# Attention and max-of-two network on one core: loading batch 0's q and k in two parts by tokens

## The chip, the cores and the metric

The kernel runs on one core of a Trainium2 chip. The metric is device time in microseconds (us), from the first to the last instruction. Most runs of a kernel agree within 0.3%. The kernel before gives 282.1 to 283.4 us in nearly all of its runs (two took 284.1); one run of 705.16 us stands alone and is not used.

Names: TensorE (PE) multiplies matrices and transposes, ScalarE (ACT) does the exponentials, VectorE (DVE) and GpSimd (POOL) copy, cast and mask, SyncE (SP) issues loads. POOL also issues loads, in the same line of instructions as its casts and masks.

## The reference, cut to what matters

```python
# q, k, v: (8 batches, 8 heads, 576 tokens, 64), each randn * 0.1
scores = (1 / sqrt(64)) * q @ k.T
mask = (row // 64) >= (col // 64)          # causal by blocks of 64
attn = softmax(where(mask, scores, -1e9)) @ v
x = attn as (4608 tokens, 512)
out = maximum(x @ w1, x @ w2) @ w_out      # w1, w2: 512 x 1024, w_out: 1024 x 512
```

With q and k scaled by 0.1, a score has a spread of about 0.1 x 0.1 x sqrt(64) / 8 = 0.01, so the softmax is nearly flat, and which token a score belongs to hardly shows in the output. "Correct" is therefore a weak statement here about the order of tokens in q and k.

## The kernel before

Heads go in pairs, pairs in groups of two; batch 0 is groups 0 and 1. One load brings q (or k) of a group, 64 x 2 partitions of 9 tokens each. It is cast to bf16, transposed on TensorE, and copied from PSUM.

```python
NP = 64; RPP = S // NP        # 9 tokens per partition
QCUT = 256                    # early queries: below token 256

def load_qk(g, queues, gated=False):
    ...
    raws[nm, g] = t = raw.tile([P, 2, RPP * D], FP32, name=f"{nm}raw")
    if gated:
        nc.gpsimd.memset(t[:, 0, :1], 0.0)      # holds the load back until POOL gets here
    queue.dma_start(out=t[:], in_=src[b, 4 * u:4 * u + 4].rearrange(
        "(s h) (p t) d -> (h p) s (t d)", h=2, t=RPP))

def load_v(b, c):   nc.gpsimd.dma_start(...)    # 128 tokens of all heads
def load_w(...):    nc.gpsimd.dma_start(...)    # columns of w1 and w2
def mask(p, a0, eng=None):
    (eng or nc.gpsimd).memset(aT_r[p % NA][BLK:, :, a0:a0 + BLK], 0.0)
def fill(n):        # n units of the first projection, as far as its tokens are done
def warm_up(n):     # n matmuls of 512 columns on zeros: nothing useful
```

The schedule of batch 0 is written out by hand. `burst_p` is the scores and exponential of a pair's early queries, `burst_q1` to `q3` of its late ones, `av` the product of attention and v (tiles 0, 1 early, 2 to 4 late), `x_out` the transposes of its result. Group 2 already belongs to batch 1.

```python
warm_up(16)
cq = transposes("q", 0, (dve, act)); ck = transposes("k", 0, (act, dve))
...
burst_p(0); masks_p(0); burst_p(1); warm_up(2); masks_p(1)
for c in range(2, NCH): load_v(0, c)            # POOL
load_w(256, 256)                                # POOL
...
cast("q", 2, ((pool, 0, RPP),)); masks_q(0); cast("k", 2, ((pool, 0, RPP),))
...
```

The softmax here doesn't subtract the row's maximum and nothing guards it: scores larger than these inputs give would overflow.

## Time and profile before

| | before |
|---|---|
| time, median | 283.12 us |
| TensorE busy | 96% of the span |
| first scores of batch 0 | 8.44 us |
| early k of group 1 cast on POOL | 9.17 us |
| attention times v, tiles 2 to 4, of pair 0 and pair 2 | 20.31 and 24.86 us |
| first scores of batch 1 | 27.06 us |

The prediction below shows the chain of waits, the stretches and the timelines. Columns: busy us and (count) of PE, weight loads, DVE, ACT and POOL, the granted clock, DMA share, GB/s.

```profile
0.00:8.30 8.30, 6.04 (x52) 2.50 (x52) 5.07 (x20) 2.76 (x5) 3.21 (x10) 1.00 0.78 281
8.30:16.00 7.70, 6.01 (x98) 3.17 (x101) 6.51 (x16) 6.06 (x10) 7.26 (x14) 1.00 1.52 258
```

Read the last column with the length of the stretch: 8.3 us at 281 GB/s are 2.33 MB, and 7.7 us at 258 are 1.99 MB, so 4.32 MB had come by 16 us.

The marks on TensorE's timeline are these (start us, busy us, then in brackets any idle time before and what ended it):

```profile
8.44 0.34 PE L321 MATMUL ps_s<-qT,kT 64*128 64x256 bf16 x4 [0.73 <-ACT kT L310]
...
20.31 0.90 PE L429 MATMUL ps_o<-vv,aT 128*128 128x65 bf16 x24
...
24.86 0.88 PE L429 MATMUL ps_o<-vv,aT 128*128 128x65 bf16 x24
...
27.06 0.61 PE L321 MATMUL ps_s<-qT,kT 64*128 64x512 bf16 x6
```

### The profile page before, as it was taken

The numbers are of one execution on the slowest core, as the hardware profiler recorded it, in microseconds if no ns is written. First come the engines' busy times: TensorE is split into PE (matmuls) and PEld (weight loads), VectorE is DVE, ScalarE is ACT, GpSimd is POOL, SyncE is SP. The second block draws the span as 40 slices with busy tenths as digits, with TensorE's granted clock in tenths as the row PEclk, the third lists the DMA queues.
The fourth block names the chain that finished last, engine by engine and source line by source line (L and its number), as shares of the span: only waits on it lengthen the run. The fifth ranks groups of instructions, "written<-read, shape, count | busy, mean of one in ns | idle before, by whom it ended". The sixth has DMA issues, their size and how long they took to land.

```text
span 280.4 us, 7767 instructions
## 1 busy us (share of the span) xinstructions
PE 269.3 (96%) x3208; PEld 151.5 (54%) x3253; DVE 185.7 (66%) x386; ACT 139.6 (50%) x194; POOL 107.7 (38%) x271
## 2 busy tenths in 40 slices
PE   7699999999999999999999999999999999999995
PEld 2356766655556455555555554646455644444543
DVE  5967879668887676767667576757655766365430
ACT  3786577667664664655647374664653000100112
POOL 2996446764654625164344625371120000000000
PEclk9999999999999999999999999999999999999999
DMA  7999999979934994479266866175301111111114
GB/s 261 263 219 220 187 244 273 250 148 189 210 42 153 154 156 78 178 82 239 49 208 77 219 75 196 52 81 50 67 5 49 49 54 40 39 75 40 73 41 150
DMA packets 55940, 36.68 MB, mean 131 GB/s; under 512 B 38752, under 2 KB 43232, under 8 KB 55904
## 3 DMA queue, kind: packets, MB, share of 16 engines
q0 software_dynamic: 41728, 7.87, 35.0%
q1 hardware_dynamic: 13760, 27.66, 28.8%
q10 hardware_dynamic: 416, 0.66, 0.7%
q8 instruction: 25, 0.41, 0.6%
q14 instruction: 11, 0.09, 0.1%
HBM read 34.60 MB, written 9.44 MB: 157 GB/s over the span
## 4 chain that ended last, share of the span: by engine, by line
PE 91%; DMA 4%; issue 2%; ACT 1%; DVE 1%; POOL 0%; ACTq 0%
PE ps_h L197 43%; PE ps_y L215 22%; PE ps_o L429 11%; PE ps_s L321 8%; DMA vv<-in_v_dram 2%; PE ps_xe L451 2%; PE ps_qT L303 2%; DMA qraw<-in_q_dram 2%; PE ps_kT L303 2%; ACT aT L345 1%; PE ps_s L339 1%; PE ps_y L231 1%; PE ps_w L292 1%; DVE g L206 0%; POOL vv L133 0%
## 5 line engine op out<-in xcount | busy, mean ns | idle before, releaser
L197 PE MATMUL ps_h<-xT,w_sb 128*128 128x512 bf16 (+3 forms) x605 | 136.2, 357 | 1.7 <-issue 0.3
L345 ACT ACTIVATE aT<-ps_s 128x1024 bf16<-128x1024 f32 (+2 forms) x100 | 96.2, 996 | 17.2 <-PE ps_s L321 16.2
L197 PEld LDWEIGHTS <-w_sb 128*128 128x128 bf16 x640 | 57.8, 98 | 57.4 <-issue 8.1
L204 DVE CAST h<-ps_h 128x512 bf16<-128x512 f32 (+3 forms) x80 | 50.9, 637 | 28.9 <-PE ps_h L197 26.7
L215 PE MATMUL ps_y<-wo_sb,g 128*128 128x512 bf16 x273 | 65.5, 379 | 2.1 <-PE ps_s L321 1.3
L206 DVE TENSOR_TENSOR g<-h,ps_h 128x512 bf16<-128x512 bf16 (+3 forms) x80 | 50.6, 632 | 12.0 <-PE ps_h L197 10.5
L350 POOL MEMSET aT<- 64x128 bf16 x124 | 22.3, 199 | 92.7 <-ACT aT L345 91.3
L221 ACT COPY y<-ps_y 128x512 f32<-128x512 f32 x31 | 18.1, 584 | 70.3 <-PE ps_y L215 56.5
L429 PEld LDWEIGHTS <-aT 128*128 128x128 bf16 x960 | 37.3, 98 | 14.1 <-issue 1.3
L215 PEld LDWEIGHTS <-g 128*128 128x128 bf16 x280 | 26.8, 98 | 30.4 <-issue 1.1
L429 PE MATMUL ps_o<-vv,aT 128*128 128x65 bf16 x960 | 39.9, 194 | 0.3 <-DMA vv<-in_v_dram 0.3
L133 POOL DMA_DIRECT2D vv<-in_v_dram x40 | 33.7, 847 | 0.5
L436 DVE TENSOR_TENSOR xp<-ps_o,rec 128x256 bf16<-128x256 f32 (+1 forms) x64 | 31.4, 491 | 2.2
L321 PE MATMUL ps_s<-qT,kT 64*128 64x64 bf16 (+6 forms) x344 | 31.6, 279 | 1.1 <-ACT kT L310 0.7
L435 DVE RECIPROCAL rec<-ps_o 128x4 f32<-128x4 f32 (+1 forms) x64 | 12.0, 188 | 20.6 <-PE ps_o L429 18.9
L310 ACT COPY qT<-ps_qT 128x576 bf16<-128x576 bf16 x15 | 9.6, 638 | 29.4 <-PE ps_qT L303 29.4
L187 POOL COPY g<-g 128x512 bf16<-128x512 bf16 x8 | 4.9, 611 | 38.3 <-DVE g L206 38.2
L129 POOL CAST kn<-kraw 128x1152 bf16<-128x1152 f32 x15 | 17.3, 1151 | 5.2 <-DMA kraw<-in_k_dram 5.1
L129 POOL CAST qn<-qraw 128x1152 bf16<-128x1152 f32 (+1 forms) x15 | 16.5, 1099 | 7.0 <-DMA qraw<-in_q_dram 6.9
L456 DVE COPY xT<-ps_xe 128x640 bf16<-128x640 bf16 (+2 forms) x18 | 8.2, 453 | 15.7 <-PE ps_xe L451 14.9
L310 ACT COPY kT<-ps_kT 128x576 bf16<-128x576 bf16 x15 | 9.6, 638 | 15.0 <-PE ps_kT L303 15.0
L321 PEld LDWEIGHTS <-kT 64*128 64x128 bf16 x344 | 13.2, 95 | 6.6 <-issue 2.8
(44 smaller groups left out, 144.5 us busy)
## 6 DMA issues: line engine op xcount, KB each, us to landing
qraw<-in_q_dram SPq DMA_DIRECT2D x16, 576.0 KB, 4.1
out_dram<-y SPq DMA_DIRECT2D x35, 256.0 KB, 2.1
kraw<-in_k_dram SPq DMA_DIRECT2D x15, 576.0 KB, 5.4
vv<-in_v_dram POOLq DMA_DIRECT2D x32, 128.0 KB, 5.3
w_sb<-in_moe_w_dram POOLq DMA_DIRECT2D x4, 256.0 KB, 6.6
w_sb<-in_moe_w_dram POOLq DMA_DIRECT2D x2, 512.0 KB, 10.7
wo_sb<-in_moe_w_out_dram POOLq DMA_DIRECT2D x2, 512.0 KB, 11.8
kraw<-in_k_dram ACTq DMA_DIRECT2D x1, 576.0 KB, 5.4
```

What stands on the lines that cost most here:

```text
L129: copy(out=n[:, j0:j1], in_=t[:, j0:j1])
L133: nc.gpsimd.dma_start(out=vv_r[b % NV][P - rows:, c, :, :D], in_=v[b, :, c * P:c * P + rows, :].rearrange("h p d -> p h d"),)
L197: nc.tensor.matmul(pt[:, :w], w_sb[:, c, f * P:(f + 1) * P], xT[:, c, t0:t0 + w], start=(c == 0), stop=(c == NDM - 1),)
L204: nc.vector.tensor_copy(out=h1[:, :w], in_=pt[:, :w])
L206: nc.vector.tensor_max(g[:, f, m:m + w], h1[:, :w], pt[:, :w])
L215: nc.tensor.matmul(py[:], g[:, f, s * P:(s + 1) * P], wo_sb[:, f, :], start=(f == 0), stop=(f == NFF - 1),)
L310: copies[i](out=t[:, :S].rearrange("q (p j) -> q p j", j=RPP), in_=pts[i].rearrange("q j p -> q p j"),)
L321: nc.tensor.matmul(ps[:, hh, col:col + w], kT[r, k0:k0 + P], qT[r, q0:q0 + w], start=True, stop=True,)
L345: nc.scalar.activation(out=aT_r[p % NA][:, :, a0:a0 + w], in_=ps[:, :, :w], func=AF.Exp, scale=scale,)
L350: (eng or nc.gpsimd).memset(aT_r[p % NA][BLK:, :, a0:a0 + BLK], 0.0)
L429: nc.tensor.matmul(po[:, gi, hh, :], a[:, hh, a0:a0 + P], vv[:, c, h0 + 2 * hh, :], start=(mm == 0), stop=(mm == n_mm - 1),)
L436: nc.vector.tensor_mul(xp[:, ts[0]:ts[0] + n, :, p % 2], po[:, :, :, :D], rec[:, :n].to_broadcast([P, n, 2, D]),)
```

## The change

The scores of the early queries need only tokens below 256. So the change loads, casts and transposes those first, and the rest later; it shortens the first warm-up from 16 to 9 matmuls and rewrites batch 0's order around the two parts. Whole loads stay for all other groups.

```diff
+    LO = (0, QCUT // NP, 0)                        # tokens below 256, 4 per partition
+    HI = (QCUT, RPP - QCUT // NP, QCUT // NP)      # the other 320, 5 per partition
 def load_qk(g, queues, gated=False, part=ALL):
+            for h in range(2):
+                queue.dma_start(
+                    out=t[h * NP:(h + 1) * NP, :, j0 * D:(j0 + n) * D],
+                    in_=src[b, 4 * u + h:4 * u + 4:2, tok:tok + n * NP].rearrange(
+                        "s (p t) d -> p s (t d)", t=n),
+                )
-    load_qk(0, (SP, ACT))
+    load_qk(0, (SP, ACT), part=LO)
-    load_qk(1, (SP, SP))
+    load_qk(1, (SP, SP), part=LO)
+    load_qk(0, (SP, SP), part=HI)
+    load_qk(1, (SP, SP), part=HI)
     load_qk(2, (SP, None))
-    cast("q", 0, ((dve, 0, 7), (pool, 7, RPP)))
-    cast("k", 0, ((act, 0, 5), (dve, 5, RPP)))
     for c in range(2):
         load_v(0, c)
-    load_w(0, 256, (0,))
-    cast("k", 1, ((pool, 0, RPP),))
-    load_w(0, 256, (1,))
-    load_qk(2, (None, SP), gated=True)
+    cast("q", 0, ((dve, 0, NLO),))
+    cast("k", 0, ((act, 0, NLO),))
+    cast("k", 1, ((pool, 0, NLO),))
+    load_w(0, 256)
 ... (transposes() likewise takes a part)
-    warm_up(16)
+    warm_up(9)
 ... (POOL now casts the four late parts; v chunks 2 to 4 move behind them and two
      more weight loads; group 2's gated k load moves behind v; v chunks 3 and 4 of
      batch 1 move ahead of the masks of pair 2; the early products move ahead of
      the late scores)
```

A part of a group no longer has a single stride over its 128 partitions, since between head parities the step in memory is that of the whole 576 tokens. Each part is therefore two loads, one for each half of the partitions.

More of the change, by code (lines that the diff above doesn't have):

```diff
@@ L109, with load_qk @@
     dve, pool, act = nc.vector.tensor_copy, nc.gpsimd.tensor_copy, nc.scalar.copy
-    def load_qk(g, queues, gated=False):
+    ALL = (0, RPP, 0)
+    LO = (0, QCUT // NP, 0)
+    HI = (QCUT, RPP - QCUT // NP, QCUT // NP)
+    def load_qk(g, queues, gated=False, part=ALL):
         b, u = divmod(g, GPB)
+        tok, n, j0 = part
         for nm, src, queue in (("q", q, queues[0]), ("k", k, queues[1])):
@@ L115, in load_qk @@
                 continue
-            raws[nm, g] = t = raw.tile([P, 2, RPP * D], FP32, name=f"{nm}raw")
+            if j0 == 0:
+                raws[nm, g] = raw.tile([P, 2, RPP * D], FP32, name=f"{nm}raw")
+            t = raws[nm, g]
             if gated:
                 nc.gpsimd.memset(t[:, 0, :1], 0.0)
-            queue.dma_start(
-                out=t[:],
-                in_=src[b, 4 * u:4 * u + 4].rearrange(
-                    "(s h) (p t) d -> (h p) s (t d)", h=2, t=RPP),
-            )
+            if part is ALL:
+                queue.dma_start(
+                    out=t[:],
+                    in_=src[b, 4 * u:4 * u + 4].rearrange(
+                        "(s h) (p t) d -> (h p) s (t d)", h=2, t=RPP),
+                )
+                continue
+            for h in range(2):
+                queue.dma_start(
+                    out=t[h * NP:(h + 1) * NP, :, j0 * D:(j0 + n) * D],
+                    in_=src[b, 4 * u + h:4 * u + 4:2, tok:tok + n * NP].rearrange(
+                        "s (p t) d -> p s (t d)", t=n),
+                )
     def cast(nm, g, parts):
-        t = raws.pop((nm, g)).rearrange("p s (t d) -> p t s d", d=D)
-        qk_n[nm, g] = n = qkn.tile([P, RPP, 2, D], BF16, name=f"{nm}n")
+        t = raws[nm, g].rearrange("p s (t d) -> p t s d", d=D)
+        if parts[0][1] == 0:
+            qk_n[nm, g] = qkn.tile([P, RPP, 2, D], BF16, name=f"{nm}n")
+        n = qk_n[nm, g]
         for copy, j0, j1 in parts:
@@ L168 @@
         nc.vector.memset(kz_r[r][:, BLK:2 * BLK], 0.0)
-    cast("q", 0, ((dve, 0, 7), (pool, 7, RPP)))
-    cast("k", 0, ((act, 0, 5), (dve, 5, RPP)))
     for c in range(2):
         load_v(0, c)
-    load_w(0, 256, (0,))
-    cast("k", 1, ((pool, 0, RPP),))
-    load_w(0, 256, (1,))
-    load_qk(2, (None, SP), gated=True)
+    NLO = QCUT // NP
+    cast("q", 0, ((dve, 0, NLO),))
+    cast("k", 0, ((act, 0, NLO),))
+    cast("k", 1, ((pool, 0, NLO),))
+    load_w(0, 256)
     done_tokens = [0]
@@ L295, with transposes @@
     xps = {}
-    def transposes(nm, g, copies):
-        n = qk_n.pop((nm, g))
-        pts = [ps_m.tile([P, RPP, NP], BF16, name=f"ps_{nm}T", tag="m") for _ in range(2)]
-        for j in range(RPP):
+    def transposes(nm, g, copies, part=ALL):
+        n = qk_n[nm, g]
+        tok, nt, j0 = part
+        pts = [ps_m.tile([P, nt, NP], BF16, name=f"ps_{nm}T", tag="m") for _ in range(2)]
+        for j in range(nt):
             for i in range(2):
@@ L303, in transposes @@
                 nc.tensor.transpose(
-                    pts[i][:, j, :], n[r, j].rearrange("p s d -> p (s d)"), ident[r, r],
+                    pts[i][:, j, :], n[r, j0 + j].rearrange("p s d -> p (s d)"), ident[r, r],
                 )
@@ L310, in copy_out @@
                 copies[i](
-                    out=t[:, :S].rearrange("q (p j) -> q p j", j=RPP),
+                    out=t[:, tok:tok + nt * NP].rearrange("q (p j) -> q p j", j=nt),
                     in_=pts[i].rearrange("q j p -> q p j"),
@@ L498, in t_pair @@
         return lambda: [f() for f in outs]
-    warm_up(16)
-    cq = transposes("q", 0, (dve, act))
-    ck = transposes("k", 0, (act, dve))
+    warm_up(9)
+    cq = transposes("q", 0, (dve, act), LO)
+    ck = transposes("k", 0, (act, dve), LO)
     cq((0,))
@@ L507 @@
     ck((1,))
-    cast("q", 1, ((dve, 0, RPP),))
+    cast("q", 1, ((dve, 0, NLO),))
     burst_p(0)
@@ L513 @@
     masks_p(1)
-    for c in range(2, NCH):
-        load_v(0, c)
+    cast("q", 0, ((pool, NLO, RPP),))
+    cast("k", 0, ((pool, NLO, RPP),))
     load_w(256, 256)
-    cq = transposes("q", 1, (dve, dve))
-    burst_q1(0)
-    ck = transposes("k", 1, (dve, dve))
+    cq = transposes("q", 1, (dve, dve), LO)
+    ck = transposes("k", 1, (dve, dve), LO)
     for i in range(2):
@@ L522 @@
         ck((i,))
-    load_w(512, 512)
-    warm_up(3)
+    cast("q", 1, ((pool, NLO, RPP),))
+    cast("k", 1, ((pool, NLO, RPP),))
+    warm_up(2)
     burst_p(2)
     av(0, [0, 1])
-    burst_q3(0)
-    warm_up(2)
+    warm_up(1)
     burst_p(3)
@@ L532 @@
     masks_p(3, nc.vector)
-    burst_q2(0)
-    av(2, [0, 1])
-    warm_up(2)
-    burst_q1(1)
-    av(3, [0, 1])
-    x_out(0, 0, 2)
-    warm_up(2)
-    cast("q", 2, ((pool, 0, RPP),))
+    for c in range(2, NCH):
+        load_v(0, c)
+    warm_up(2)
+    av(2, [0, 1])
+    transposes("q", 0, (act, act), HI)()
+    x_out(0, 0, 2)
+    av(3, [0, 1])
+    burst_q1(0)
+    warm_up(2)
+    x_out(1, 0, 2)
+    load_qk(2, (None, SP), gated=True)
+    load_w(512, 256)
+    burst_q1(1)
+    transposes("k", 0, (dve, dve), HI)()
+    fill(2)
+    burst_q2(0)
+    transposes("q", 1, (act, dve), HI)()
+    fill(2)
+    load_w(768, 256)
+    burst_q3(0)
     masks_q(0)
-    cast("k", 2, ((pool, 0, RPP),))
     burst_q2(1)
-    x_out(1, 0, 2)
-    warm_up(2)
+    fill(2)
+    transposes("k", 1, (dve, dve), HI)()
     burst_q3(1)
     masks_q(1)
+    cast("q", 2, ((pool, 0, RPP),))
+    cast("k", 2, ((pool, 0, RPP),))
+    fill(2)
     for c in range(3):
         load_v(1, c)
+    burst_q1(2)
+    av(0, [2, 3, 4])
     fill(2)
     load_qk(3, (SP, SP), gated=True)
-    burst_q1(2)
+    burst_q1(3)
+    av(1, [2, 3, 4])
+    fill(2)
     transposes("q", 2, (dve, act))()
-    fill(3)
     burst_q2(2)
-    av(0, [2, 3, 4])
-    fill(1)
+    fill(2)
+    for c in range(3, NCH):
+        load_v(1, c)
+    x_out(0, 2, NCH)
     burst_q3(2)
     masks_q(2)
-    for c in range(3, NCH):
-        load_v(1, c)
-    av(1, [2, 3, 4])
+    burst_q2(3)
     fill(2)
-    burst_q1(3)
     transposes("k", 2, (dve, act))()
@@ L567 @@
     pad_keys(5)
-    fill(2)
-    x_out(0, 2, NCH)
-    burst_q2(3)
     av(2, [2, 3, 4])
-    fill(2)
     burst_q3(3)
```

## The prediction

> **What bounds the kernel now.** I read the page first: the chain of work that ended last, then busy time in stretches that I cut at the kernel's own stages, then the timeline of TensorE (PE) and of GpSimd (POOL) in the first 28 us, because the change touches nothing later. The chain, by engine:
>
> ```profile
> PE 91%; DMA 4%; issue 2%; ACT 1%; DVE 1%; POOL 0%; ACTq 0%
> ```
>
> So the end is set by PE's work plus the time in which PE has nothing useful to do. The stretches are: before the first transposes, the ragged start, the rest of batch 0's own schedule, the batches up to 70 us, the remainder. The columns are busy us and (count) for PE, weight loads, DVE, ACT, POOL, then the granted clock, DMA share and GB/s:
>
> ```profile
> 0.00:6.90 6.90, 5.23 (x16) 1.87 (x16) 3.68 (x18) 2.20 (x3) 1.81 (x8) 1.00 0.73 258
> 6.90:16.00 9.10, 6.83 (x134) 3.80 (x137) 7.90 (x18) 6.62 (x11) 8.66 (x16) 1.00 1.45 279
> 16.00:27.06 11.06, 10.74 (x205) 7.30 (x205) 8.09 (x24) 8.44 (x12) 9.54 (x21) 1.00 1.67 190
> 27.06:70.00 42.94, 42.20 (x668) 27.62 (x674) 33.61 (x76) 30.10 (x40) 24.52 (x66) 1.00 1.16 218
> 70.00:280.40 210.40, 204.33 (x2201) 110.89 (x2232) 132.47 (x254) 92.26 (x131) 63.16 (x164) 1.00 0.46 99
> ```
>
> From 27.06 us PE is 98% busy with work that must be done. The change can only move the moment at which the first scores of batch 1 (at 27.06 us) start, and the amount of the first projection already done by then. Before it, 6.9 us hold only warm-up matmuls, and between 6.9 and 27.06 us PE is idle 2.6 us and spends about 3.2 us in 13 more warm-up matmuls (my sum over the timeline). The ceiling is thus about 12 us, and the realistic part much less. POOL is 95% and 86% busy in the second and third stretch (8.66 of 9.10, 9.54 of 11.06), and the DMA share is above 1: those two are the suspects for what holds PE in the start.
>
> ```profile
> 5.76 1.09 DVE L129 CAST qn<-qraw 128x896 bf16<-128x896 f32 x1 [1.60 <-DMA qraw<-in_q_dram]
> 6.91 0.44 PE L303 MATMUL ps_qT<-ident,qn 64*128 64x64 bf16 x18 [0.44 <-DVE qn L129]
> 8.44 0.34 PE L321 MATMUL ps_s<-qT,kT 64*128 64x256 bf16 x4 [0.73 <-ACT kT L310]
> ...
> 14.15 3.01 POOL L145 DMA_DIRECT2D w_sb<-in_moe_w_dram  x4
> 17.20 1.14 POOL L129 CAST qn<-qraw 128x1152 bf16<-128x1152 f32 x1
> 18.40 0.34 POOL L350 MEMSET aT<- 64x128 bf16 x2
> 18.81 1.15 POOL L129 CAST kn<-kraw 128x1152 bf16<-128x1152 f32 x1
> 20.01 0.34 POOL L350 MEMSET aT<- 64x128 bf16 x2
> 20.30 2.64 POOL L133 DMA_DIRECT2D vv<-in_v_dram  x3
> ...
> 23.19 0.34 POOL L350 MEMSET aT<- 64x128 bf16 x2
> 23.47 1.57 POOL L133 DMA_DIRECT2D vv<-in_v_dram  x2
> ```
>
> The reader should see two things. First, load, cast, transpose, copy: q lands at 5.76, first scores at 8.44. Second, POOL issues the loads of v and of the weights itself, 0.75 to 0.9 us each, in one line with casts and with the mask memsets (line 350). The masks of pair 0's late queries end at 18.74 us, and its attention-times-v for tiles 2 to 4 starts at 20.31; pair 2's masks end at 23.53, and its product runs at 24.86. These masks had 1.3 us to spare, so POOL is nearly as late as PE needs it.
>
> **What the Trainium skill says.** "SBUF — State Buffer", section "Door 1: The DMA port swizzle", says that partitions 0 to 63 reach only 8 of 16 ports, measured at 196 GB/s against 328 for 128 partitions, and the section on issuing two DMAs for both halves says that they serialize, a gain of only 6%. The new loads are of exactly this form, 64 partitions each. This trace has no such q or k load; its 128-partition loads run at about 400 GB/s (DMA view, 4 to 6 us). "PSUM — Partial Sum Buffer", section "Engine vs sequencer instructions", says that ScalarE, VectorE and GpSimd queues are strict FIFO; the trace agrees, since POOL sat 4.48 us before the q cast at 5.79 and only then issued v. "TensorE: Matmul & The Clock Gate", Part 1, says warm-up takes some 3.4 us of time, not a count of matmuls; here weight loads come every 0.43 us until 4.58 us and faster afterwards, 3.3 us after the first at 1.24. Nine warm-up matmuls reach 4.8 us, so they should just suffice.
>
> **The change part by part.**
>
> *Start.* The first 0.52 MB (q and k below token 256) replace 1.18 MB. From 0.75 us the old pair needed until 5.7 and 6.2. Data flow from about 2.2 us; at the full 400 GB/s the new pair lands at about 4.2, at half rate about 5.2; I take 4.9. A cast of 128x512 takes 0.60 (the k cast on DVE had this form). Eight transposes instead of 18 and copies of 256 columns for 576 (0.76 to about 0.37 us) put the first scores at about 6.6 instead of 8.44: 1.8 us earlier. Eleven fewer warm-up matmuls (29 to 18) remove filler only.
>
> *More casts, copies and loads.* Copies out of PSUM go from 8 of 576 to 8 of 256 and 8 of 320: 8 more fixed costs of 0.05 us or so, but ACT now gets three of them. Its exponentials of batch 0 are 4 x (0.77+1.02+1.02+0.49) = 13.2 us in either version, so ACT does not become the bound: from 6.9 us it would end near 22 even with gaps.
>
> *POOL.* It now issues v's first two chunks during its old idle time (1.9 us off its line), but takes four casts of 128x640 (interpolated between 0.40 us for 256 and 1.15 for 1152: 0.72 each, 2.9 in all) for batch 0's late tokens, and k's early cast is 0.61 instead of 1.15. Its line starts when the early k of group 1 lands. That is the sixth load on SyncE's queue, 1.05 MB in all: about 5.5 us at full rate, 7.4 at half; I take 6.8. Then, in the changed program's order: cast 0.61, two weight loads 1.53, four masks 0.62, two casts 1.44, two weight loads 1.53, two casts 1.44, three v loads 2.44 (16.4 us); gate memset 0.1, four weight loads 3.0 (19.5); masks of pair 0 end at 19.9 against 18.74, of pair 1 at 20.2. The q cast of group 2 ends at 21.4. Group 2's k load is gated at 16.4 instead of 11.0 us; it took 6.3 us before beside the same weight traffic, so it lands at 22.7 and its cast ends at 23.9. Three v loads of batch 1, 2.64 (26.5); memsets 0.1; two v loads 1.57, now placed ahead of pair 2's masks (28.2); those masks end at 28.5, against 23.53.
>
> *PE.* From masks at 19.9 its order holds two products of 24 matmuls (0.75 each), two of 18 transposes, scores and four fills (0.45 each), by my sum 5.8 us: it reaches pair 2's product at about 25.7 and waits there to 28.5. The product, the last scores and a fill of three units take 1.7: batch 1's first scores at 30.2, not 27.06. But the new order has fills of 19 units by then against 15; a unit is two 256-column matmuls, and 16 of those took 1.99 us, so 4 units are 1.0 us already done. Sum: +3.1 - 1.0 = +2.1 us. If k of group 2 lands by 21.4, the wait for it goes away, 1.3 us less: +0.8. If POOL is not the last one anywhere, PE's 25.7 plus 1.7 gives 27.4, and the net is -0.7; with an early landing too (1 us sooner), about -1.7.
>
> **The rivals.** (1) Everything simply shifts with the first scores, 1.8 us earlier, and the dropped gaps in warm-up give another 1: 280 us. For it: PE idles in the start for want of q and k (0.44 and 0.73 us waits), and the schedule has visibly been rearranged to fill gaps. Against: POOL's occupancy. (2) The halves serialize and every load lands later; POOL's line slips another us and the result is +3: 286. For it: the skill's figure; against: POOL needs the late parts only near 10 to 14 us, so half-rate is partly hidden. (3) The weights bind: they had landed just in time (the last pair issued at 16.45 us took 11.9, landing at 28.3, while its use starts within a microsecond or two). The new order asks for them earlier, but v's head start empties the same queue sooner, so I expect them about 4 us earlier and no wait. (4) Attention's v chunks 2 to 4 are issued 1.5 to 2 us later, behind two more weight loads; they landed at 20.5 us just as they were used. A wait here would coincide with that for the masks, and adds nothing.
>
> **Range and chances.** The two fast runs of before are 282.26 and 283.12, mean 282.7. My sums give -1.7 to +3, with the centre of the reckoning near +1.3; I shade it to +0.7 because the order looks hand-tuned for this split. That gives 283.4 us, range 280.8 to 285.8. A gain of over 2% (5.7 us) would need nearly half of the whole start to vanish; a loss of that size would need PE's wait to double. So: faster 0.02, same 0.94, slower 0.04.
>
> **What would show it right or wrong.** Right: first scores near 6.6 us; q and k parts moving at well under 400 GB/s; masks of pair 0 near 19.9 and of pair 2 near 28 us; PE idle for one to three us just before pair 2's product; batch 1's first scores at 28.5 to 30 us. Wrong: POOL idle or ahead of PE around 20 to 28 us, batch 1's first scores before 27 us with 19 units filled; or a low clock after the short warm-up, seen as 0.43 us spacing of matmuls after 5 us.

## The result, and the profile after

Median 291.49 us (290.2 to 291.77, four runs) against 283.18 for the kernel before. The ratio is 1.0296 with a 95% interval of 1.0251 to 1.034: slower. Ratios here and below are the mean time of one kernel's fast runs over that of the kernel before's fast runs of the same rounds, so not quite the ratio of the medians quoted. The result is 8.4 us above the 283.12 us of the table before, 8.1 above the 283.4 that was predicted, and outside the predicted range.

The chain of waits, by engine, of the kernel after:

```profile
PE 87%; DMA 5%; POOL 2%; SPq 2%; ACT 2%; issue 1%; DVE 0%; POOLq 0%; ACTq 0%
```

PE fell from 91 to 87%, while SyncE's issuing (SPq) and POOL appear. The stretches of the first 27 us, same columns as before:

```profile
0.00:8.30 8.30, 5.31 (x33) 2.03 (x33) 3.72 (x19) 2.89 (x6) 2.60 (x8) 1.00 1.07 138
8.30:16.00 7.70, 6.29 (x59) 2.52 (x57) 3.54 (x14) 2.99 (x4) 5.34 (x11) 1.00 1.14 244
...
6.90:16.00 9.10, 7.22 (x73) 3.00 (x69) 4.29 (x16) 3.78 (x6) 5.34 (x11) 1.00 1.22 232
16.00:27.06 11.06, 8.82 (x126) 4.96 (x125) 5.91 (x17) 6.86 (x10) 8.87 (x16) 1.00 1.54 217
```

POOL, 8.66 us busy from 6.9 to 16 in the kernel before, is busy 5.34: it stands idle where it had been full. And the queues delivered 138 and 244 GB/s in the first two stretches instead of 281 and 258: 3.02 MB by 16 us, not 4.32. They were not idle, as the DMA share of over 1 shows. They were slow.

POOL's timeline shows what it waited for:

```profile
1.67 1.90 POOL L152 DMA_DIRECT2D vv<-in_v_dram  x2 [0.35 <-DVE vv L184]
10.55 0.61 POOL L148 CAST kn<-kraw 128x512 bf16<-128x512 f32 x1 [6.98 <-DMA kraw<-in_k_dram]
...
17.47 2.45 POOL L152 DMA_DIRECT2D vv<-in_v_dram  x3
...
22.98 0.44 POOL L371 MEMSET aT<- 64x128 bf16 x2
...
27.41 1.15 POOL L148 CAST kn<-kraw 128x1152 bf16<-128x1152 f32 x1 [1.49 <-DMA kraw<-in_k_dram]
...
33.69 0.52 POOL L371 MEMSET aT<- 64x128 bf16 x2 [0.91 <-ACT aT L366]
```

It stood 6.98 us before the early k cast of group 1 and began it at 10.55, where I had taken 6.8. From there to the masks of pair 0 its line ran as reckoned. And TensorE:

```profile
7.62 0.82 PE L342 MATMUL ps_s<-qT,kT 64*128 64x256 bf16 x8 [0.46 <-ACT kT L331]
8.37 1.03 PE L312 MATMUL ps_w<-zeros 128*128 128x512 bf16 x2
...
24.57 0.52 PE L450 MATMUL ps_o<-vv,aT 128*128 128x65 bf16 x9
26.26 0.43 PE L450 MATMUL ps_o<-vv,aT 128*128 128x65 bf16 x9 [1.17 <-DMA vv<-in_v_dram]
27.67 0.49 PE L450 MATMUL ps_o<-vv,aT 128*128 128x65 bf16 x6 [0.98 <-DMA vv<-in_v_dram]
...
34.87 0.90 PE L450 MATMUL ps_o<-vv,aT 128*128 128x65 bf16 x24
...
36.65 0.61 PE L342 MATMUL ps_s<-qT,kT 64*128 64x512 bf16 x6
```

Three things stand here. The first scores come at 7.62, earlier than before, but by less than half of what I expected. The product of pair 0 starts 4.26 us later than before and then waits twice for v, 2.15 us together, not for masks: the chain shows the last chunk issued at 19.21 us and landing 8.41 us later. And two warm-up matmuls at 8.37 take 1.03 us, where two of them take 0.59 us at 15.01 in the kernel before: TensorE runs at half its clock, in the spacing of its matmuls, although the clock column says 1.00. (At 13.27 us one such matmul takes 0.62 us and at 14.57 two take 1.04, so one more adds 0.42; in the kernel before it is 0.38 at 13.62 and 0.59 at 15.01, so 0.21.) The first scores of batch 1 come at 36.65, 9.6 us after those of before, with 38 matmuls of the first projection done instead of 30 (8 of them are 1.0 us): 8.6 us, close to the 8.4 us of the loss. So the loss lies before that point, as the prediction assumed.

### The profile page after: what moved, and what is told of

It reads as the page before. It is cut to its first block, busy times and chain, and to the rows that moved or that the text cites. A ratio compares the mean times of both kernels' runs of the same rounds, so it can differ in the third digit from the quotient of the medians.

```text
span 289.8 us, 7823 instructions
## 1 busy us (share of the span) xinstructions
PE 278.5 (96%) x3242; PEld 153.1 (53%) x3242; DVE 183.8 (63%) x390; ACT 140.2 (48%) x197; POOL 111.3 (38%) x276
## 4 chain that ended last, share of the span: by engine, by line
PE 87%; DMA 5%; POOL 2%; SPq 2%; ACT 2%; issue 1%; DVE 0%; POOLq 0%; ACTq 0%
PE ps_h L217 43%; PE ps_y L235 21%; PE ps_o L450 10%; PE ps_s L342 7%; DMA vv<-in_v_dram 3%; DMA qraw<-in_q_dram 2%; PE ps_qT L324 2%; PE ps_kT L324 2%; PE ps_xe L472 2%; SPq L136 2%; ACT aT L366 1%; POOL w_sb L164 1%; PE ps_s L360 1%; PE ps_y L251 1%; POOL vv L152 1%
## 5 line engine op out<-in xcount | busy, mean ns | idle before, releaser
L217 PE MATMUL ps_h<-xT,w_sb 128*128 128x512 bf16 (+3 forms) x640 | 142.7, 360 | 0.1
L366 ACT ACTIVATE aT<-ps_s 128x1024 bf16<-128x1024 f32 (+1 forms) x100 | 96.1, 997 | 23.4 <-PE ps_s L342 22.7
L235 PE MATMUL ps_y<-wo_sb,g 128*128 128x512 bf16 x280 | 66.5, 379 | 0.0
L450 PEld LDWEIGHTS <-aT 128*128 128x128 bf16 x960 | 38.6, 99 | 16.9 <-issue 3.4
L450 PE MATMUL ps_o<-vv,aT 128*128 128x65 bf16 x960 | 41.6, 196 | 2.1 <-DMA vv<-in_v_dram 2.1
L342 PE MATMUL ps_s<-qT,kT 64*128 64x64 bf16 (+6 forms) x344 | 33.0, 289 | 1.3 <-ACT aT L366 0.8
L457 DVE TENSOR_TENSOR xp<-ps_o,rec 128x256 bf16<-128x256 f32 (+1 forms) x64 | 31.4, 491 | 2.2
L331 ACT COPY qT<-ps_qT 128x576 bf16<-128x576 bf16 (+2 forms) x18 | 10.5, 588 | 32.3 <-PE ps_qT L324 32.3
L148 POOL CAST kn<-kraw 128x1152 bf16<-128x1152 f32 (+2 forms) x17 | 18.1, 1067 | 10.6 <-DMA kraw<-in_k_dram 10.1
L148 POOL CAST qn<-qraw 128x1152 bf16<-128x1152 f32 (+1 forms) x16 | 17.5, 1096 | 2.5 <-PE ps_h L217 2.4
L331 ACT COPY kT<-ps_kT 128x576 bf16<-128x576 bf16 (+1 forms) x15 | 9.3, 620 | 15.5 <-PE ps_kT L324 15.5
```

Of the source, the lines that this page charges most:

```text
L148: copy(out=n[:, j0:j1], in_=t[:, j0:j1])
L217: nc.tensor.matmul(pt[:, :w], w_sb[:, c, f * P:(f + 1) * P], xT[:, c, t0:t0 + w], start=(c == 0), stop=(c == NDM - 1),)
L235: nc.tensor.matmul(py[:], g[:, f, s * P:(s + 1) * P], wo_sb[:, f, :], start=(f == 0), stop=(f == NFF - 1),)
L331: copies[i](out=t[:, tok:tok + nt * NP].rearrange("q (p j) -> q p j", j=nt), in_=pts[i].rearrange("q j p -> q p j"),)
L342: nc.tensor.matmul(ps[:, hh, col:col + w], kT[r, k0:k0 + P], qT[r, q0:q0 + w], start=True, stop=True,)
L366: nc.scalar.activation(out=aT_r[p % NA][:, :, a0:a0 + w], in_=ps[:, :, :w], func=AF.Exp, scale=scale,)
```

## The experiments

Eighteen kernels ran, each judged correct, each beside the kernel before on the same chip, in three rounds. The figure in brackets is the median of the kernel before. Kernels are best compared by how far each lies above its own bracket; the changed kernel lay 8.3 us above.

**Is it the form of the loads?** These two change nothing in the kernel before but how the whole q and k of groups 0 and 1 are loaded: cut by partitions or cut by columns.

```diff
 b_half:
+ for h in range(2):
+     queue.dma_start(out=t[h * NP:(h + 1) * NP], in_=src[b, 4 * u + h:4 * u + 4:2] ...)
 b_cols:
+ for c0, c1 in ((0, 4 * D), (4 * D, RPP * D)):
+     queue.dma_start(out=t[:, :, c0:c1], in_=whole[:, :, c0:c1])
```

> The kernel before, with each whole load of q and k of groups 0 and 1 issued as two loads of 64 partitions (packets stay 2304 B, nothing else changes). Theory 1, the half-partition form is slow: the queue moves about 240 GB/s between 3 and 9 us instead of 400, the first q cast starts near 7 us instead of 5.8, k of group 1 is cast near 11 to 12 us instead of 9.2, and the time is 2 to 4 us longer. Rival, the size of the packets or the number of loads is what costs: 400 GB/s as before, casts within 0.7 us of before, time within 1 us.

> The kernel before, with the same whole loads each issued as two loads of all 128 partitions, by columns, so that packets are 1024 and 1280 B as in the changed kernel. Theory 1: about 400 GB/s as before, casts within 0.7 us of before, time within 1 us. Rival, small packets or more loads: about 240 GB/s, k of group 1 cast near 11 to 12 us, time 2 to 4 us longer.

Measured: b_half 288.52 us [282.56], ratio 1.0194 (1.015 to 1.0238). b_cols 284.25, ratio 1.005 (1.0016 to 1.0085). The stretch of b_half from 3.9 to 8.7 us, and then POOL's early k cast of group 1 on its timeline:

```profile
3.90:8.70 4.80, 3.61 (x11) 1.13 (x9) 1.12 (x7) 0.02 (x1) 0.67 (x2) 1.00 1.05 225
```

```profile
13.73 1.15 POOL L137 CAST kn<-kraw 128x1152 bf16<-128x1152 f32 x1 [2.45 <-DMA kraw<-in_k_dram]
```

The same views of b_cols:

```profile
3.90:8.70 4.80, 4.40 (x47) 1.75 (x45) 2.46 (x9) 1.09 (x2) 2.32 (x4) 1.00 1.08 371
```

```profile
10.09 1.15 POOL L135 CAST kn<-kraw 128x1152 bf16<-128x1152 f32 x1 [0.72 <-DMA kraw<-in_k_dram]
```

Equal bytes, and an equal number of loads: 225 against 371 GB/s, and a cast at 13.73 against 10.09 (9.17 in the kernel before). b_cols even has the smaller packets, 1024 and 1280 bytes, as in the changed kernel. So it is the 64-partition form that is slow, not the number or the size of the pieces. By itself this form costs the kernel before 6.0 us by the medians, more than the 2 to 4 expected; TensorE also runs at half clock there (two warm-up matmuls take 1.04 us at 12.76 in b_half, 0.60 at 9.84 in b_cols), and what that adds is not separated. It doesn't yet say how much of the changed kernel's loss it is, since that kernel was reordered.

**The same question from the other side.** The changed kernel with whole loads for the first two groups, and all else kept. Its casts then read columns that hold other tokens than the schedule takes them for, so the result is wrong.

```diff
-    load_qk(0, (SP, ACT), part=LO)
+    load_qk(0, (SP, ACT))
-    load_qk(1, (SP, SP), part=LO)
-    load_qk(0, (SP, SP), part=HI)
-    load_qk(1, (SP, SP), part=HI)
+    load_qk(1, (SP, SP))
```

> The changed kernel with whole loads of q and k of groups 0 and 1 (four loads as before, tokens then lie where the parts don't expect them, so the result is wrong on purpose); casts, transposes, order and all else as changed. Theory 1, the form of the loads makes most of the loss: GpSimd's first early k cast starts at 9.5 us or sooner instead of 10.55, the late casts never wait, batch 1's first scores move from 36.7 to 30 to 33 us, time 284 to 288. Rival, the new order on GpSimd and the late v loads make it: casts move by about 1 us, and the time stays at 289 to 291.

Measured: 289.81 us [282.56], ratio 1.0254 (1.0214 to 1.0293). That is 7.3 us above the kernel before, about 1 us won, within the intervals: the time is the one that I had written down for the rival, not for the theory. The profiled run is the fastest of the four (288.94); in it 3.73 MB come by 16 us and batch 1 starts at 34.08. But the early k cast is still at 10.28, because all of k is waited for, and the product of pair 2 now waits 0.89 us for POOL's masks, at 32.36. A faster load uncovers the next wait, so this run alone doesn't give the price of the form.

**Is it the short warm-up?**

```diff
-    warm_up(9)
+    warm_up(16)
```

> The changed kernel with 16 warm-up matmuls instead of 9. Theory 3, the short warm-up leaves TensorE at half clock and that costs: matmuls of 512 columns come every 0.22 us from 8 us on, and the time falls by 1 us or more. Theory 1: TensorE waits for data and GpSimd in that stretch anyway, so faster matmuls change the time by less than 0.5 us.

Measured: 291.58 us [282.56], ratio 1.0315 (1.0273 to 1.0358), no gain. The clock is then full until about 13 us and low afterwards, and the product of pair 0 waits longer for v, 1.57 and 1.78 us. What the clock gives is lost at the next load.

**Is it v's head start, or the order at the head of POOL's line?** a_vlater issues v's first two chunks after the early k cast, a_wfirst the first weight loads before it.

```diff
 a_vlater:
-    for c in range(2): load_v(0, c)          # ahead of the early casts
     cast("k", 1, ((pool, 0, NLO),))
+    for c in range(2): load_v(0, c)
 a_wfirst:
-    cast("k", 1, ((pool, 0, NLO),))
     load_w(0, 256)
+    cast("k", 1, ((pool, 0, NLO),))
```

> The changed kernel with v's first two chunks issued after the early k cast of group 1 again, not ahead of it. If v's small packets (256 B) in the way of the early loads make GpSimd's line start late, the early k cast starts at 8.5 to 9.5 us instead of 10.55; the first product with v then waits for v to about 15 to 16 us instead of 12.95, so the time moves by less than 1.5 us either way. If they do not, the cast stays at 10.3 to 10.8 and the time grows by 1.5 us or more from v alone.

> The changed kernel with the first two weight loads issued before the early k cast, in GpSimd's idle time. If GpSimd's line after 10.55 us is what the rest waits for, everything on it comes 1.5 us sooner and the time falls by 1 to 2 us (289.5 to 290.5); if the two transfers push the early k back as much as they gain, or the line is not the bound, the change is under 0.5 us.

Measured: a_vlater 292.05 us [282.69], ratio 1.0329 (1.028 to 1.0377); a_wfirst 292.59, ratio 1.0346 (1.0319 to 1.0372). With v out of the way the early k cast starts at 7.93; so v's head start, which I counted as free, cost it 2.6 us. From 4.5 to 8 us q and k moved 0.88 MB here, and 0.33 MB in the changed kernel, where 0.24 MB of v came beside them. But then the products stand for v. TensorE's timeline in a_vlater:

```profile
15.10 0.33 PE L450 MATMUL ps_o<-vv,aT 128*128 128x65 bf16 x3 [4.07 <-DMA vv<-in_v_dram]
17.22 0.32 PE L450 MATMUL ps_o<-vv,aT 128*128 128x65 bf16 x3 [1.80 <-DMA vv<-in_v_dram]
```

In a_wfirst the cast slips to 11.70, as weights now move beside k.

**The early part over all partitions.** Both heads' tokens below 256 fit two per partition over 128 partitions, in packets of 512 bytes. The late parts stay half loads. Tokens are right.

```diff
+ if part is LO:
+     queue.dma_start(out=lo[:], in_=src[b, 4 * u:4 * u + 4, :QCUT].rearrange(
+         "c (p t) d -> p c (t d)", t=2))
```

> The changed kernel with the early part loaded over all 128 partitions, two tokens of four heads each (512 B packets), one load per tensor instead of two; result meant to be right. Theory 1 (64 partitions reach half the bandwidth): q's early cast starts at 4.5 to 5.3 us instead of 6.06, the early k cast of group 1 at 7.5 to 9 instead of 10.55, and the time falls by 1.5 to 3 us. If the packets of 512 B or v's are what slows it, the casts move by less than 0.7 us and the time by less than 1 us.

Measured: 290.86 us [282.69], ratio 1.0287 (1.0264 to 1.031). The early casts come at 4.39 (q) and 6.89 (k of group 1), the latter 3.7 us before the changed kernel's and where the prediction had it. Yet TensorE waits 2.00, 1.89 and 2.08 us for v and 1.2 us for weights, batch 1 starts at 36.05, and the time is not the 1.5 to 3 us shorter that was expected. Only 3.31 MB had come by 16 us.

**The two waits at the end of the start.** a_vsooner issues v chunks 2 to 4 before the late casts. a_k2only issues group 2's gated k load early and puts pair 2's masks ahead of batch 1's last v loads. a_both does both.

```diff
 a_vsooner:
     masks_p(1)
+    for c in range(2, NCH): load_v(0, c)
     cast("q", 0, ((pool, NLO, RPP),))
 ... (its old place goes)
 a_k2only:
     load_w(0, 256)
+    load_qk(2, (None, SP), gated=True)
 ...
     masks_q(2)
+    for c in range(3, NCH): load_v(1, c)
 ... (their old places go)
```

> The changed kernel with v chunks 2 to 4 issued before the late casts of group 0 and the second pair of weight loads, as the kernel before had them. If the wait for v that the trace shows at 25 to 27.6 us carries the loss, the last of them lands at 21 to 23 us instead of 27.6, batch 1's first scores come 2 to 3.5 us sooner, and the time is 288 to 289.5. If the masks or the late casts bind right behind (they move 2.4 us later), the gain is under 1 us.

> The changed kernel with group 2's k load gated early again and pair 2's masks ahead of batch 1's last v loads, as in the kernel before; v chunks 2 to 4 stay late. If two waits stand side by side (v's late chunks for pair 0, pair 2's masks behind the gated k cast), taking only the second away gains little: 290 to 292 us, batch 1's first scores at 35.5 to 37. If the masks alone carried it, 287 to 289.

> Both together: v chunks 2 to 4 sooner, group 2's k gated early, pair 2's masks ahead of the last v loads. Two waits side by side: each alone gained nothing, both together bring batch 1's first scores from 36.5 to 31 to 33 us and the time to 286 to 288. If something else binds (transfers of the whole start, or the clock), it stays at 289.5 or more.

Measured: a_vsooner 291.24 us [282.69], ratio 1.0299 (1.0269 to 1.033); a_k2only 291.06 [282.53], 1.0303 (1.0277 to 1.0329); a_both 289.51 [282.53], 1.0269 (1.0205 to 1.0332). In a_vsooner there is no wait for v, and this on TensorE's timeline, then on POOL's:

```profile
33.41 1.39 PE L450 MATMUL ps_o<-vv,aT 128*128 128x65 bf16 x22 [2.86 <-POOL aT L371]
```

```profile
27.74 1.15 POOL L148 CAST kn<-kraw 128x1152 bf16<-128x1152 f32 x1 [2.54 <-DMA kraw<-in_k_dram]
28.83 2.65 POOL L152 DMA_DIRECT2D vv<-in_v_dram  x3
31.52 1.60 POOL L152 DMA_DIRECT2D vv<-in_v_dram  x2
33.15 0.34 POOL L371 MEMSET aT<- 64x128 bf16 x2
```

This is the wait that the prediction built its sum on, link by link: the gated k load lands late, v's loads of batch 1 stand ahead, the masks come last, the product waits. In the changed kernel it is hidden behind the wait for v. The two are of like length, 2.86 us here and 2.15 there, and taking one away alone changes nothing: without the wait for v the masks hold, and in a_k2only the wait for v is down to 1.16 us but waits for weights of 1.71 and 0.89 us come before it, with batch 1 at 35.98. With both away the first scores of batch 1 come at 33.14 instead of 36.65, in the fastest of a_both's four runs (288.58). The medians say 2.0 us, though a_both's own interval is too wide to tell it from the other two, and 289.5 is where the expectation put "something else binds". The closer figure is that of a_both16 below: 6.3 us above its kernel before, where a_warm16, with the same warm-up, lies 9.0 above (ratios 1.0233 and 1.0315, intervals apart). So the two waits together are worth about 2.7 us.

**Both waits away, and faster loads too.** w_both is a_both with a_whole's edit (tokens wrong), lo_both is a_both with a_lo128's.

> The same order as the kernel with both, with whole loads of 128 partitions (wrong result on purpose). If the 64-partition loads cost time once the order no longer hides it, this is 2 to 4 us faster than the kernel with both, 282.5 to 285.5; if they do not matter for the end, the two agree within 1 us.

> The same order with the early part loaded over 128 partitions (right result). Its early casts end 2 to 3.5 us sooner, so GpSimd's line moves by as much: 283.5 to 286. If the software queue of v and weights binds instead, as the waits of 2 us for v in the run with only this change suggest, it is no faster than the kernel with both.

Measured: w_both 287.42 us [282.53], ratio 1.0171 (1.0125 to 1.0218); lo_both 289.02, ratio 1.0231 (1.0202 to 1.0259). w_both, expected at 282.5 to 285.5, has moved 4.09 MB by 16 us and starts batch 1 at 32.21. lo_both has moved 3.31 and starts it at 35.26: POOL casts k at 6.70 and comes to the weights early, and TensorE then waits 1.88 us for them and 1.58 for v.

**What is left: clock or order?** b_warm9 is the kernel before with `warm_up(9)` for `warm_up(16)`; w_both16 and a_both16 are w_both and a_both with `warm_up(16)` for `warm_up(9)`.

> The kernel before with one number changed: the first warm-up has 9 matmuls instead of 16. Theory (the half clock has a price of its own): TensorE stays at 0.43 us for 512 columns well past 7 us, the first scores of batch 1 come 1.5 us or more after 27.06, and the time is 1.5 to 4 us above before. Rival (hidden under GpSimd's line, which sets the pace until 24 us in before): within 0.8 us of before. Second rival: q still comes late, so the idle gap after the short warm-up is longer than in the changed kernel, and the clock is low for longer than 21 us: over 4 us.

> w_both (whole loads with the tokens wrong on purpose, v chunks 2 to 4 sooner, group 2's k gated early, pair 2's masks first) with 16 warm-up matmuls instead of 9. Theory (with the waits for data mostly gone, the half clock from 7 to 21 us is what is left): full clock from about 7 us on, the first scores of batch 1 at about 30 instead of 32.2, and 2 to 3 us less than w_both's 287.4, so about 285. Rival (what is left is GpSimd's order, the clock being hidden under it): within 0.8 us of w_both, and TensorE waits longer instead, for masks or v.

> a_both (the changed kernel with v chunks 2 to 4 sooner, group 2's k gated early and pair 2's masks first) with 16 warm-up matmuls instead of 9. Theory (half clock is what is left): 1.5 to 3 us less than a_both's 289.5, so about 287, and first scores of batch 1 at about 31 instead of 33.1. Rival (hidden under waits for loads): within 0.8 us of a_both, as the same edit did nothing to the changed kernel itself.

Measured: b_warm9 283.17 us [282.87], ratio 1.0021 (0.9998 to 1.0044); w_both16 286.65, ratio 1.0126 (1.0096 to 1.0156); a_both16 289.15, ratio 1.0233 (1.0213 to 1.0252). The short warm-up alone does leave the kernel before at half clock: two warm-up matmuls take 1.03 us at 9.28 and 0.60 again at 13.40. It costs it 0.6 us, not surely different from nothing, since TensorE's marked idle time between 8.3 us and batch 1 shrinks from 2.4 to 1.7 us meanwhile. In w_both the longer warm-up wins 0.8 us by the medians, in a_both 0.4 (1.1 and 0.7 against the kernel before); the intervals overlap. So the rival holds: the clock is real and nearly free here. The two kernels with the long warm-up also give the cleanest price of the loads, since their intervals are apart: whole loads (w_both16) against half loads (a_both16) are 2.5 us faster. Form and number go together in that figure, 4 whole loads against 16 half ones.

In w_both16 the start still waits for data, in these places on TensorE's timeline:

```profile
12.18 0.27 PE L449 MATMUL ps_o<-vv,aT 128*128 128x65 bf16 x3 [0.66 <-POOL aT L370]
12.89 0.25 PE L449 MATMUL ps_o<-vv,aT 128*128 128x65 bf16 x3 [0.44 <-DMA vv<-in_v_dram]
...
15.76 0.32 PE L323 MATMUL ps_qT<-ident,qn 64*128 64x64 bf16 x10 [1.23 <-POOL qn L148]
...
17.19 0.97 PE L311 MATMUL ps_w<-zeros 128*128 128x512 bf16 x2
...
31.95 0.61 PE L341 MATMUL ps_s<-qT,kT 64*128 64x512 bf16 x6
```

Its idle time in brackets from 8.3 us to batch 1 is 4.35 us, against 2.44 in the kernel before, and it ran at half clock once more after those waits, from about 17 to 20.5 us (two warm-ups in 0.97 us instead of 0.60; four matmuls of the projection in 1.04 instead of 0.61). I estimate its price at about 1 us, from the excess of the matmuls there over the same forms later. The first scores of batch 1 are 4.9 us later than in before with 1.0 us more filled; the waits (1.9) and the clock (1) are three quarters of those 3.9. Not all of its loss lies before batch 1: from there to the next scores of this form it takes 11.72 us against 11.03 in before, with a wait of 0.77 us for POOL's cast at 37.71. The late casts, which POOL alone does in the new order, are one of the waits.

**Right tokens over all partitions, in both parts.** These cut each part by pair instead of by head parity: still two loads for a part, but each over 128 partitions. s_both has a_both's edits too, and s_both16 the long warm-up.

```diff
- for h in range(2):
-     queue.dma_start(out=t[h * NP:(h + 1) * NP, :, cols], in_=... "s (p t) d -> p s (t d)")
+ for s in range(2):
+     queue.dma_start(out=t[:, s, cols], in_=... "h (p t) d -> h p (t d)")
```

> The changed kernel with each part's two loads cut by pair (s) instead of by head parity (h): still two loads for each part, the right tokens, the same packets of 1024 and 1280 bytes, but each over all 128 partitions. Theory (64 partitions move at 215 to 240 GB/s, and that is what starves the start): over 350 GB/s from 9 to 11 us, 3.7 MB or more moved by 16 us instead of 3.02, group 1's early k cast at 7.5 to 9 us instead of 10.55, and 1.5 to 2.5 us less than the changed kernel, about 289.5, as in a_whole, since the waits for v's last chunks and for pair 2's masks stay. Rival (the number of loads and v's small packets starve it): cast still after 10 us, within 0.8 us of 291.5.

> a_both (v chunks 2 to 4 sooner, group 2's k gated early, pair 2's masks first) with the loads of a_s128. All tokens right, so it is the honest form of w_both. Theory (load rate plus the two waits): 3.9 MB or more by 16 us, first scores of batch 1 near 31.5, time 286.5 to 287.5. Rival (w_both gained because it had fewer loads, eight instead of sixteen, not because of the partitions): within 0.8 us of a_both's 289.5. If the earlier first scores count too (early parts land at 4.5, not with the whole load at 6), it could reach 285.5; under 282 I do not expect it.

> s_both with 16 warm-up matmuls instead of 9. Theory (the clock is a minor term): 0 to 1.3 us less than s_both, as between w_both and w_both16. Rival (with early data and early clock together the start finally runs ahead): 3 us less, at or under before's 282.8.

Measured: 335.44, 335.88 and 335.53 us [282.49], ratio 1.1892 (1.1864 to 1.192) for the first. A clear miss of every expectation. The stretch of s_both from 8.3 to 16 us:

```profile
8.30:16.00 7.70, 0.00 (x0) 0.00 (x0) 0.00 (x0) 0.62 (x1) 0.00 (x0) 1.00 0.16 39
```

39 GB/s: nothing else runs, and the queues themselves are almost idle. The Trainium skill offers the explanation: "DMA: Bandwidth & Descriptors", section "Why a DMA increments its semaphore by 16 and not by 1", says that a load runs on the largest number of engines up to 16 that divides the slowest dimension of both its sides. My source pattern starts with the two head parities, so the number is 2. The trace agrees in the rate: 39 to 48 GB/s are about an eighth of the 371 to 410 that loads over 128 partitions reach here. It has no view of the single engines. I had this page at hand and didn't apply it. So these three runs answer another question than the one that I asked, and a correct two-part load at full rate has not been made.

No experiment beats the kernel before.

## Why the prediction was wrong

What had come by 16 us sums the experiments up:

| kernel | loads of groups 0 and 1 | MB by 8.3 us | MB by 16 us | batch 1 starts | median us |
|---|---|---|---|---|---|
| before | whole | 2.33 | 4.32 | 27.06 | 283.12 |
| b_half | whole, by halves | 1.41 | 3.23 | | 288.52 |
| after | two parts, by halves | 1.15 | 3.02 | 36.65 | 291.49 |
| a_vlater | the same | 1.45 | 3.18 | 37.23 | 292.05 |
| a_vsooner | the same | 1.13 | 3.04 | 36.40 | 291.24 |
| a_lo128 | late part by halves | 1.51 | 3.31 | 36.05 | 290.86 |
| a_both | two parts, by halves | 1.15 | 3.25 | 33.14 | 289.51 |
| w_both | whole (wrong tokens) | 2.21 | 4.09 | 32.21 | 287.42 |

Every kernel with half loads has 3.0 to 3.3 MB by 16 us, whatever its order. A reordering then only chooses which consumer stands: k (after), v (a_vlater, a_lo128) or weights (lo_both). Where whole loads bring the 4 MB, what remains is the order and, a little, the clock.

Point by point, by the prediction's own steps:

- *"First scores at about 6.6."* Measured 7.62. Right in kind: the early part does come first. The early q was cast at 6.06 where landing at 4.9 was taken.
- *"About 5.5 us at full rate, 7.4 at half; I take 6.8"* for the early k of group 1. **This is the step that failed.** Measured 10.55. The mechanism had been quoted (64 partitions, two halves that serialize), but I set a value below that of half rate. The sum was also uneven: its 5.5 is 2.2 us, plus 1.05 MB at 400 GB/s, plus about 0.7; with the same 0.7, half rate gives 8.1, and a_vlater has 7.93.
- *What that figure left out.* Of the 3.75 us, v's two chunks account for 2.62: 7.93 without them (a_vlater). "During its old idle time (1.9 us off its line)" counted what it takes to issue v and not its traffic. From 4.5 to 8 us 1962 of 2280 packets were under 512 bytes (v's are some 125 bytes by this count, not the 256 of the expectation) and all queues moved 162 GB/s, so the sum of 1.05 MB at half rate left out 0.26 MB of v that goes in small packets. The loads account for as much from their side: the same bytes over 128 partitions, in half as many loads, bring the cast to 6.89 even beside v (a_lo128). The two don't add: 2.62 and 3.66 are more than 3.75.
- *Form or issue?* Issuing is a rival that no run separates from the form in the changed kernel: a half load takes SyncE 0.61 us where a whole one took 0.46, and the sixth ends at 5.0 us. Half loads of 160 KB every 0.65 us can't pass 252 GB/s (my estimate from these two numbers), and a_vlater's q and k moved at 251 from 4.5 to 8 us.
- *Behind it stood the assumption that the slow loads delay this cast alone.* It failed too: putting the cast right doesn't put the time right. In a_lo128 it starts at 6.89, and the kernel still takes 290.86 us, with 6 us of waits for v and 1.2 for weights in its place. All of these loads come beside each other, and together they had brought 3.0 to 3.3 MB by 16 us in the kernels with half loads, where the kernel before had 4.32.
- *POOL's line from there on.* Right. From the early cast to the end of v's issue 9.6 us were predicted, 9.37 measured; to the end of pair 0's masks 13.1 and 12.87. The whole line stood 3.75 us late at its head and 3.5 at those masks (23.42 against 19.9).
- *Pair 2's masks make the product wait.* The mechanism is right and is seen in a_vsooner, link by link; in the kernel after it is hidden.
- *Rival 4, that a wait for v "would coincide with that for the masks, and adds nothing".* Right about the time, as far as the runs show: without it (a_vsooner) nothing is gained, because the masks' 2.86 us then show. But the wait came, 2.15 us, in an earlier product, and it took the place of the masks' wait. Both away (a_both) starts batch 1 3.5 us earlier.
- *"Nine warm-up matmuls ... should just suffice."* Wrong in this profile, small in effect. The half clock lasted to about 20.9 us. It is not the same in every run: with the same nine, a_vsooner's profile has the full clock at 8.10 us (two warm-ups in 0.60) and half at 11.98 (1.04). Its price measured by itself is 0.2% (b_warm9), 0.8 us in w_both, neither sure.
- *Rival 3, weights as the bound.* Not in the kernel after. Waits for weights appear in a_lo128, a_k2only and lo_both, where something else got ahead of the weights, and one of 0.78 us in a_warm16.
- *"POOL needs the late parts only near 10 to 14 us, so half-rate is partly hidden"*, the argument against rival 2. It failed: the late parts' traffic isn't hidden, since v and weights come beside it (162 GB/s for q, k and v together from 4.5 to 8 us). Rival 2's +3 was the right branch, and too small.
- *The fill credit.* Right: 8 matmuls more, 1.0 us.
- *The shading from +1.3 to +0.7* "because the order looks hand-tuned for this split" rested on nothing in the profile.

The sum in the prediction's terms: batch 1 was due at 30.2 and came at 36.65, 6.45 us more. The product of pair 0 began 4.67 us later than its 19.9. POOL's line accounts for 3.5 of that (the masks end at 23.42); TensorE itself got there 1.15 us after the masks, without a marked wait. From there to pair 2's product 8.6 us were reckoned, 2.8 of them mask wait, and 10.3 measured, with 2.15 of v wait instead and a half clock from 27.6 to 31.4 us. That makes 4.67 + 1.7 = 6.4.

In sum, with the long warm-up the time above the kernel before goes from 9.0 us (a_warm16) to 6.3 without the two waits (a_both16), and to 3.8 with whole loads as well (w_both16). What stays open: how that rest, 3.8 us in w_both16 and 4.9 in w_both, divides between POOL's late casts, the order of the products and the clock (w_both16 accounts for about three quarters of what is left there by marked waits and clock, partly by estimate); what share of the loads' price the issue alone has; and whether a correct two-part load at full rate would make this schedule pay.

## What to carry to other kernels

Before a load is split, look at what the split does to its form on both sides: which partitions it covers, and what its outermost dimension is. Half the partitions cost the kernel before 6 us, and an outermost dimension of two cost the changed kernel another 44. Then add up the bytes that all queues must have delivered by each consumer's time, and price an early load by what it delays; if the sum doesn't fit, reordering only moves the wait. And where two waits stand side by side, test them together: each alone looked innocent.

## What the Trainium skill lacked or had wrong

- "SBUF — State Buffer", section "Can I just issue two DMAs to hit both halves?": right, and more binding than I read it. The runs add the figure for two loads in flight, one on each half: 225 GB/s together (b_half), where the same bytes over all partitions moved at 371 (b_cols). Its figure for issuing, some hundreds of ns, doesn't tell one form of load from another: a half load took SyncE 0.61 us, a whole one 0.46.
- "DMA: Bandwidth & Descriptors": its rule on the number of engines fits (39 to 48 GB/s for a source whose outermost dimension is 2). What I missed in it is a figure for what small packets do to the loads beside them: with v's packets, 1962 of 2280 under 512 bytes, all queues together moved 162 GB/s, against 251 in the same stretch of a_vlater, where v had not been issued.
- "TensorE: Matmul & The Clock Gate", table under "Why this matters for your kernels": warm up with at least 4 us, and no gaps above some 3 us. Keeping to both was not enough in these profiles. In the changed kernel 4.02 us of warm-up and then 1.29 us without work were followed by half the clock until about 20.9 us (in a_vsooner, with the same nine matmuls, it was still full at 8.10), and in w_both16, after 16 warm-up matmuls, waits of at most 1.23 us, several in a row, were followed by half clock again. The page has such a case under "A second HAM failure mode", for another pattern of work; here the gaps are waits for data, and that they are the cause is not shown.
